# Moving DMA issue, weight casts and eviction copies between engines in the Q and K stage of a fused attention and Mish block

## The chip, the cores and the metric

The kernel runs on one core of a Trainium2 chip. The metric is the device time of one execution in microseconds (us). Engines are named as in the profile: PE (TensorE, matmuls), PEld (its weight loads), DVE (VectorE), ACT (ScalarE), POOL (GpSimd) and SP (SyncE, which only issues transfers). SPq and ACTq are the sequencers of SP and ACT, where DMA issues appear.

## The reference

The input x is 2048 x 1024. It is normalised by row, and two branches use the result:

```
x  = A_x
xn = layernorm(x)
s  = attention(xn, A_wqkv, 32 heads of 32) @ A_wo
h  = xn @ B_w1 + B_b1                  # 1024 -> 3584
g  = silu((h * tanh(softplus(h))) @ B_w2)   # 3584 -> 1024
out = x + s * g
```

All inputs are float32.

## The kernel before

**Precision.** A matmul in one pass of float32r is not exact enough, so operands are split into a high part (a copy that rounds to float32r) and a low part (the value minus its high part). The helper `copy` (line 275) makes a high part on ACT, `low` (line 282) the low part on the engine that it is given, and `THREE` (line 286) is the list of the three products high x high, high x low, low x high that are added up in PSUM. `move` (line 278) issues a DMA, on SP unless it is given another engine.

**Stages.** First the rows of x are normalised, transposed and split, and V is made, with the first splits of W1 beside it. Then comes the Q and K stage, where the change lies. Then a planner (`Plan`, line 84) lays out by costs the instructions of attention and of the two dense layers; its order doesn't depend on the run. Last comes the output projection.

**The Q and K stage** is the loop at line 709. The 16 values of f are 128-column blocks of the Q and K weights, in turn Q and K; c runs over four blocks of 512 rows. `qk_group(f, c)` (line 692) is a *group*: 24 matmuls (8 slices of 128 by `THREE`) into one PSUM tile `ps` of one bank, out of eight banks; the high part copied out to `qst`, the low part subtracted from it on DVE, and a store of 512 KB to the DRAM tensors `qs` or `ks`. Groups are numbered here from 0 to 63 as 4f + c.

The weights of a block are loaded by `qk_load(f)` (line 478) into `qkraw` (one buffer), and split by `qk_split(f)` (line 484), which calls `split_w` (line 348), into `qkw` (two buffers in turn). The split of block f + 1 is put after group (f, 0), and the load of block f + 2 right after that.

From f = 12, each group is followed by four score matmuls of head 0 (`s_mm`, line 580), each with a bank of its own and a maximum on DVE (line 586); `m_tail` (line 590) turns the maxima into rows of the Q operand. Head 0's Q and K are loaded at f = 8, head 1's at f = 15 (`load_head`, line 562).

**The work beside it.** A list `todo` holds splits of weights that the dense layers need later: `presplit` (line 632) for the last blocks of W1, and `w2_parts` (line 657) for W2. W2 is split for a fast product with seven combinations of four quarters: per double block u there are four steps with 2, 2, 2 and 1 combinations. `minus` forms a combination on POOL where one is needed (four times per u), and `w2_part` (line 651) casts and subtracts on POOL into a tile `pw`, which is stored by SP one tick later. The list of 108 units of work is laid out by a due group, `cost / PACE`, so many units per group; the loop takes what is due after each group. `later` holds what is to be issued some groups (ticks) later. `pw_tile` (line 627) takes tiles in turn from two places, three buffers each.

Each engine, and each DMA queue, works in the order in which the program issues to it. In this stage ACT issues the stores of `qst` and the loads of `qkraw` (from f = 2); SP issues everything else.

Of the kernel before, what the change touches and what calls it, by code (L numbers as in the profile page):

```python
# [10 lines left out]
F32R = mybir.dt.float32r  # L11
# [7 lines left out]
P = 128  # L19
# [6 lines left out]

W1_0, W1_V = 4, 23

PACE = 1.85
NS = H * NT  # L30
U = FT // 2

# [191 lines left out]
def body(ctx: ExitStack, tc: tile.TileContext, x, wqk, wv, wo, w1, b1, w2, out):  # L224
    nc = tc.nc
# [6 lines left out]
    def pool(stack, name, bufs, side="left", **kw):  # L232
        return stack.enter_context(tc.tile_pool(name=name, bufs=bufs, side=side, reuse_waits="tile", **kw))
# [9 lines left out]
    w2s = [dram.tile([P, 7, 2, 512], F32R, name=f"w2s{i}") for i in range(U)]  # L243
# [25 lines left out]
    w1p = pool(low_, "w1p", 1)  # L269
# [5 lines left out]
    def copy(out_, in_, scale=1.0):  # L275
        nc.scalar.activation(out_, in_, AF.Copy, scale=scale)  # L276

    def move(out_, in_, eng=None):

        (eng or nc.sync).dma_start(out_.bitcast(F32), in_.bitcast(F32))  # L280

    def low(eng, out_, in_, high):

        eng.tensor_tensor(out_, in_, high.bitcast(F32), ALU.subtract)  # L284
# [10 lines left out]
    later = Later()  # L295
# [52 lines left out]
    def split_w(w, raw, job=False):  # L348
        for half in range(2):
            r = slice(half * 4, half * 4 + 4)  # L350
            p = w[half] if isinstance(w, list) else w[:, half]
            if job:
                nc.gpsimd.tensor_copy(p[:, 0], raw[:, r])
            else:
                copy(p[:, 0], raw[:, r])
            low(nc.gpsimd if job else nc.vector, p[:, 1], raw[:, r], p[:, 0])

    def w1_first(n, step):
        t, g = xc[2 + n // 2], n % 2
        raw = first_w1[n // 2][:, g]  # L360
        w = t[:, 1, 4 * g:4 * g + 4].rearrange("p k n -> p (k n)") \
            .rearrange("p (h a k f) -> p h a k f", h=2, a=2, f=P)
        if step == 0:
            nc.sync.dma_start(raw, w1[n])
        elif step == 1:
            split_w(w, raw, True)
        else:
            move(w1s[n], w)
# [75 lines left out]
    for t in range(2, NT + 2):  # L444
# [22 lines left out]
        if t > 7:  # L467
            c, k = t // 4 - 1, t % 4 * 2
# [7 lines left out]
    raws = {}  # L476

    def qk_load(f):
        raws[f] = big.tile([P, KT, P], F32, tag="raw", name=f"qkraw{f}")
        (nc.scalar if f > 1 else nc.sync).dma_start(raws[f], wqk[f])  # L480

    qkw = {}

    def qk_split(f):
        qkw[f] = w_tile(f"qkw{f}")
        split_w(qkw[f], raws.pop(f))
# [4 lines left out]
    def w1_early(step):  # L491
        f, late = W1_0 + step // 2, step % 2
        if not late:
            if f < W1_V:
                raw = vp.tile([P, KT, P], F32, tag="x", name=f"w1e{f}", bufs=5)
                nc.sync.dma_start(raw, w1[f])
                early_w1[f] = raw
            if W1_0 < f <= W1_V:
                f -= 1
                raw = early_w1.pop(f)  # L500
                if f % 3 == 2:
                    w = [w1p.tile([P, 2, KT // 2, P], F32R, tag="w1", name=f"w1h{f}_{i}", bufs=3) for i in range(2)]
                    split_w(w, raw, True)
                    early_w1[f] = [(w1s[f][:, i], w[i]) for i in range(2)]
                else:
                    w = w_tile(f"w1p{f}")
                    split_w(w, raw, True)
                    early_w1[f] = [(w1s[f], w)]
        elif W1_0 < f <= W1_V:
            for args in early_w1.pop(f - 1):  # L510
                move(*args)

    for i in range(1, 4):
        vw = nvw
        for t in range(NT):
            v_group(i, vw, t)()
            w1_early((i - 1) * NT + t)
            if t == 4 and i < 3:
                nvw = v_split(i + 1, vraw)
                if i < 2:  # L520
                    vraw = v_load(i + 2)
            if i == 3 and t == 1:
                qk_load(0)
            if i == 3 and t == 7:
                qk_split(0)
                qk_load(1)
# [6 lines left out]
    qst, kst = [], []  # L533
# [88 lines left out]
    sp = pool(qb, "sp", 2, side="right")  # L622
    jobs = iter([(f, half) for f in range(W1_V, FT) for half in range(2)])

    pw_made = []

    def pw_tile(name):
        pw_made.append(name)
        where, tag = ((w1p, "w1"), (sp, "pw"))[len(pw_made) % 2]
        return where.tile([P, 2, 512], F32R, tag=tag, name=name, bufs=3)  # L630

    def presplit():
        f, half = next(jobs)
        raw = sp.tile([P, 512], F32, tag="praw", name=f"praw{f}_{half}", bufs=1)
        nc.sync.dma_start(raw.rearrange("p (k f) -> p k f", f=P), w1[f][:, half * 4:half * 4 + 4])

        def split():
            w = pw_tile(f"pw{f}_{half}")
            nc.gpsimd.tensor_copy(w[:, 0], raw)
            low(nc.gpsimd, w[:, 1], raw, w[:, 0])  # L640
            later.at(1, lambda: move(w1s[f][:, half], w.rearrange("p a (k f) -> p a k f", f=P)))

        later.at(2, split)
# [3 lines left out]
    def w2_load(u):  # L647
        raw2[u] = early.tile([P, 4, 512], F32, tag=f"{'qk'[u % 2]}stack1", name=f"raw2_{u}")
        nc.sync.dma_start(raw2[u].rearrange("p (f d) n -> p f (d n)", f=2), w2[u])

    def w2_part(u, j, v):
        w = pw_tile(f"pw2_{u}_{j}")
        nc.gpsimd.tensor_copy(w[:, 0], v)
        low(nc.gpsimd, w[:, 1], v, w[:, 0])
        later.at(1, lambda: move(w2s[u][:, j], w))

    def w2_parts(u, step):
        b11, b12, b21, b22 = [raw2[u][:, i] for i in range(4)]
        if step == 0:
            raw2[u, "t"] = sp.tile([P, 512], F32, tag="tmp2", name=f"tmp2_{u}", bufs=1)  # L660
        tmp = raw2[u, "t"]

        def minus(a, b, out_):
            nc.gpsimd.tensor_tensor(out_, a, b, ALU.subtract)
            return out_

        if step == 0:
            w2_part(u, 0, b11)
            w2_part(u, 2, b21)
        elif step == 1:  # L670
            w2_part(u, 5, minus(b12, b11, tmp))
            w2_part(u, 1, minus(b22, b12, b12))
        elif step == 2:
            w2_part(u, 4, minus(b22, tmp, tmp))
            w2_part(u, 6, b22)
        else:
            w2_part(u, 3, minus(b21, tmp, tmp))

    todo, cost = [], 0.0
    for u in range(U):  # L680
        for step, n in enumerate((2, 2, 2, 1)):
            def job(u=u, step=step):
                w2_parts(u, step)
                if step == 3 and u + 2 < U:
                    later.at(1, lambda: w2_load(u + 2))
            todo.append((cost / PACE, job))
            cost += n
        if u < 2 * (FT - W1_V):
            todo.append((cost / PACE, presplit))
            cost += 1  # L690

    def qk_group(f, c):
        w = qkw[f]
        ps = ps1.tile([P, 512], F32, tag="ps", name=f"qk{f}_{c}")
        n = 0
        for k in range(KT):
            for a, b in THREE:
                nc.tensor.matmul(ps, w[:, k // 4, a, k % 4], xc[c][:, b, k], start=n == 0, stop=n == 3 * KT - 1)  # L698
                n += 1
        st = sp.tile([P, 2, 512], F32R, tag="qst", name=f"qst{f}_{c}")  # L700
        copy(st[:, 0], ps)
        low(nc.vector, st[:, 1], ps, st[:, 0])
        dst = (qs, ks)[f % 2][f // 2].rearrange("h p n -> p h n")[:, :, c * 512:(c + 1) * 512]
        move(dst, st, nc.scalar)

    w2_load(0)
    w2_load(1)
# [1 line left out]
    for f in range(2 * KT):  # L709
        for c in range(NC):  # L710
            qk_group(f, c if f < 2 * KT - 1 else (c + 1) % NC)
            while todo and todo[0][0] <= f * NC + c:
                todo.pop(0)[1]()
            if c == 0 and f + 1 < 2 * KT:
                qk_split(f + 1)
                if f + 2 < 2 * KT:
                    later.at(1, lambda f=f + 2: qk_load(f))
            if f == 8 and c == 0:
                load_head(0)
            if f == 15 and c == 0:  # L720
                stacks(early, 1)
                load_head(1)
            if f >= 12:
                for kc in range(4):
                    s_mm(0, 4 * (f - 12) + c, kc)
            if f == 2 * KT - 1 and c == 1:
                load_w1(0)
                load_w1(1)
            later.tick()
# [489 lines left out]
    wt, ohl, ps, wo_loads, wo_ops, o_ops, o_first = {}, {}, {}, {}, {}, {}, []  # L1219
# [250 lines left out]
```

## Time and profile before

| | |
|---|---|
| median of three runs | 3464.68 us (3463.0 to 3465.96) |
| the profiled execution | 3463.9 us |
| its span in the trace | 3462.1 us |
| mean granted PE clock | 0.992 |
| busy over the span | PE 97%, POOL 81%, DVE 76%, ACT 58% |
| moved by DMA | 639.92 MB, mean 185 GB/s |

The span is the time from the first to the last instruction on the core; 1.8 us of the execution lie outside it. The Q and K stage takes about an eighth of it. Its rows are shown where the argument uses them. In a row of the waits the numbers are the total in us, how often, and the longest; the arrow points to what ended the wait. In a row of an instruction group they are the busy time, the mean ns of one, and the idle time just before them with its releasers. In the order of time they are start and duration in us.

### The profile page before, as it was taken

To read this page: it belongs to the slowest core of one execution; us is meant where nothing else is said; L and a number is where in the kernel's file an instruction comes from. 1 tells how busy PE (TensorE), PEld (TensorE's weight loads), DVE (VectorE), ACT (ScalarE), POOL (GpSimd) and SP (SyncE) were. 2 spreads that over 40 slices of the span, in tenths; PEclk is the share of its full clock that TensorE was granted. 3 is DMA by queue.
4 is the path that set the end of the run, shared out by engine and by line. 5 is a ranking of instruction groups with operands and counts; after the bars stand their busy time and mean duration, and the time that the engine had idled before them with its cause. 6 is when DMAs were issued, how large, how long until landed. Compare 5 with 4: busy or idle time off the path is not lost. (4 is left out here: it accounts for less than half of the span.)

```text
span 3462.1 us, 48685 instructions
## 1 busy us (share of the span) xinstructions
PE 3371.6 (97%) x17491; PEld 2473.6 (71%) x17491; DVE 2619.2 (76%) x4382; ACT 2020.3 (58%) x3360; POOL 2792.6 (81%) x1033
## 2 busy tenths in 40 slices
PE   8999898999999999999999999999999999999999
PEld 7998676767776666667677676666676666667687
DVE  6011214799999998888989988898999889996753
ACT  6111111576776666767767667676676676677621
POOL 2669891589888888989889889989988999999910
PEclk9999999999999999999999999999999999999999
DMA  9889994444555556545445654445545545556582
GB/s 333 326 302 348 343 354 160 139 139 135 153 155 152 156 157 204 153 138 151 143 144 157 191 178 146 128 141 151 154 147 189 177 135 154 151 159 192 167 307 85
DMA packets 255477, 639.92 MB, mean 185 GB/s; under 512 B 90026, under 2 KB 99242, under 8 KB 244906
## 3 DMA queue, kind: packets, MB, share of 16 engines
q1 hardware_dynamic: 233364, 587.52, 54.3%
q10 hardware_dynamic: 21872, 49.29, 3.8%
q8 instruction: 139, 2.28, 0.3%
q14 instruction: 102, 0.84, 0.1%
HBM read 474.97 MB, written 160.69 MB: 184 GB/s over the span
## 5 line engine op out<-in xcount | busy, mean ns | idle before, releaser
L889 POOL TENSOR_TENSOR z<-z,p 128x2048 f32<-128x2048 f32 x448 | 2067.0, 4614 | 76.3 <-ACT p L273 51.4
L273 ACT ACTIVATE p<-t,zero 128x512 f32<-128x512 f32 x2048 | 1366.6, 689 | 459.7 <-PE t L860 439.4
L779 DVE TENSOR_REDUCE mx<-s 128x1 f32<-128x512 f32 x1984 | 1284.0, 682 | 70.2 <-PE s L773 67.5
L860 PE MATMUL t<-qstack,kstack 128*128 128x512 f32 x2048 | 791.5, 394 | 4.4 <-DMA qstack<-mt 2.7
L773 PE MATMUL s<-kstack,qstack 128*128 128x512 f32 x1984 | 755.8, 397 | 15.6 <-DMA kstack<-ks 5.9
L1019 PE MATMUL h<-xr,w 128*128 128x512 f32 x2016 | 678.3, 391 | 1.4 <-DVE aw L284 0.6
L1183 DVE TENSOR_TENSOR yacc<-yacc,y 128x512 f32<-128x512 f32 x728 | 492.6, 680 | 38.9 <-PE y L1160 35.7
L773 PEld LDWEIGHTS s<-kstack,qstack 128*128 128x128 f32 x1984 | 367.4, 188 | 161.5 <-issue 29.4
L860 PEld LDWEIGHTS t<-qstack,kstack 128*128 128x128 f32 x2048 | 381.7, 188 | 129.4 <-issue 31.6
L908 PE MATMUL pv<-p,v 128*32 128x512 f32 x4096 | 466.6, 596 | 0.9 <-ACT p L273 0.6
L1019 PEld LDWEIGHTS h<-xr,w 128*128 128x128 f32 x2016 | 378.7, 188 | 84.6 <-DVE aw L284 2.1
L698 PE MATMUL qk<-xc,qkw 128*128 128x512 f32 x1536 | 362.5, 397 | 20.8 <-ACT qkw L276 18.6
L698 PEld LDWEIGHTS qk<-xc,qkw 128*128 128x128 f32 x1536 | 294.1, 192 | 86.4 <-ACT qkw L276 20.3
L889 POOL TENSOR_TENSOR z<-p,p 128x2048 f32<-128x2048 f32 x32 | 147.8, 4619 | 237.9 <-ACT p L273 130.5
L908 PEld LDWEIGHTS pv<-p,v 128*32 128x32 f32 x4096 | 120.0, 110 | 276.8 <-issue 247.5
L284 DVE TENSOR_TENSOR qst<-qk,qst 128x512 fp32r<-128x512 f32 x64 | 44.3, 692 | 261.5 <-ACT qst L276 261.5
L1160 PE MATMUL y<-w,az 128*128 128x512 f32 x672 | 232.6, 396 | 4.0 <-DMA w<-w2s 2.6
L1160 PE MATMUL y<-w,ay 128*128 128x512 f32 x672 | 228.4, 393 | 3.3 <-ACT ay L276 1.3
L1160 PE MATMUL y<-w,ax 128*128 128x512 f32 x672 | 225.4, 392 | 2.8 <-DVE ax L284 0.7
L276 ACT ACTIVATE qst<-qk 128x512 fp32r<-128x512 f32 x64 | 38.3, 599 | 321.5 <-PE qk L698 118.7
L1019 PE MATMUL h<-xc,w 128*128 128x512 f32 x672 | 224.9, 390 | 0.7 <-DVE mx L586 0.7
L331 PE MATMUL v<-vw,xc 128*128 128x256 f32 x1536 | 192.9, 286 | 5.9 <-DVE xc L284 3.7
(123 smaller groups left out, 3664.3 us busy)
## 6 DMA issues: line engine op xcount, KB each, us to landing
w<-w2s SPq DMA_DIRECT2D x392, 512.0 KB
w<-w1s SPq DMA_DIRECT2D x224, 512.0 KB
w2s<-pw SPq DMA_DIRECT2D x98, 512.0 KB
qstack<-qs SPq DMA_DIRECT2D x96, 256.0 KB
kstack<-ks SPq DMA_DIRECT2D x96, 256.0 KB
x<-in_A_x_dram SPq DMA_DIRECT2D x32, 512.0 KB
qs<-qst ACTq DMA_DIRECT2D x32, 512.0 KB
ks<-qst ACTq DMA_DIRECT2D x32, 512.0 KB
```

The source lines that it names most:

```text
L273: nc.scalar.activation(out_, in_, fn, bias=zero if bias is None else bias, scale=scale)
L284: eng.tensor_tensor(out_, in_, high.bitcast(F32), ALU.subtract)
L331: nc.tensor.matmul(ps[:, :256], xc[t // 4][:, a, k, (t % 4) * P:(t % 4 + 1) * P], w[:, b, k], start=n == 0, stop=n == 3 * KT - 1)
L698: nc.tensor.matmul(ps, w[:, k // 4, a, k % 4], xc[c][:, b, k], start=n == 0, stop=n == 3 * KT - 1)
L773: nc.tensor.matmul(sp_, qst[h % 3][:, qt * P:(qt + 1) * P], kst[h % 3][:, kc * 512:(kc + 1) * 512], start=True, stop=True)
L779: nc.vector.reduce_max(tiles["mx"][:, qt, kc:kc + 1], tiles[qt, kc], axis=AX.X)
L860: nc.tensor.matmul(tp, kst[h % 3][:, kt * P:(kt + 1) * P], qst[h % 3][:, c * 512:(c + 1) * 512], start=True, stop=True)
L889: nc.gpsimd.tensor_tensor(zs[h], pts[T - 1] if kt == 1 else zs[h], pts[T], ALU.add)
L908: nc.tensor.matmul(t["b"][c * DH:(c + 1) * DH, :], vt[h][:, k, :], pts[T - kt + k][:, c * 512:(c + 1) * 512], start=k == kt - size + 1, st ...
L1019: nc.tensor.matmul(t["h"], w1t[m_][:, a, k % 4], xts_[c][:, b, k], start=i == 0, stop=i == 3 * KT - 1)
L1160: nc.tensor.matmul(t["y"], acts[B, kind][:, p, half * 256 + s * P:half * 256 + (s + 1) * P], w2t[m_][:, q], start=i == 0, stop=i == 2)
L1183: nc.vector.tensor_tensor(ya, ya, t["y"], ALU.subtract)
```

## The change

In the Q and K stage:

- ACT issues no DMA: the stores of `qst` and all loads of `qkraw` go to SP's queue.
- `split_w` outside the early jobs makes the high parts of the Q and K weights on DVE instead of ACT; the low parts were on DVE already.
- The high part of a group's output is copied out by DVE for f below 12, and by ACT, as before, from f = 12.
- The high parts of W2's combinations, and of the W1 blocks in `presplit`, are made by ACT instead of POOL. POOL keeps the combinations and the low parts. Within a step of W2, all combinations and high parts are now put out before the low parts; step 2 does its two combinations in the other order.
- `qst` has three buffers instead of two. The tiles `pw` have five instead of six: two in one place, three in the other.
- `PACE` is 1.9 instead of 1.85, and the due times start at a cost of 2 instead of 0.

```
-PACE = 1.85
+PACE = 1.9
...
-            if job:
-                nc.gpsimd.tensor_copy(p[:, 0], raw[:, r])
-            else:
-                copy(p[:, 0], raw[:, r])
+            (nc.gpsimd if job else nc.vector).tensor_copy(p[:, 0], raw[:, r])
             low(nc.gpsimd if job else nc.vector, p[:, 1], raw[:, r], p[:, 0])
...
-        (nc.scalar if f > 1 else nc.sync).dma_start(raws[f], wqk[f])
+        nc.sync.dma_start(raws[f], wqk[f])
...
-        where, tag = ((w1p, "w1"), (sp, "pw"))[len(pw_made) % 2]
-        return where.tile([P, 2, 512], F32R, tag=tag, name=name, bufs=3)
+        where, tag, bufs = ((w1p, "w1", 3), (sp, "pw", 2))[len(pw_made) % 5 % 2]
+        return where.tile([P, 2, 512], F32R, tag=tag, name=name, bufs=bufs)
...
             w = pw_tile(f"pw{f}_{half}")
-            nc.gpsimd.tensor_copy(w[:, 0], raw)
+            copy(w[:, 0], raw)
             low(nc.gpsimd, w[:, 1], raw, w[:, 0])
...
-    def w2_part(u, j, v):
+    def w2_high(u, j, v):
         w = pw_tile(f"pw2_{u}_{j}")
-        nc.gpsimd.tensor_copy(w[:, 0], v)
-        low(nc.gpsimd, w[:, 1], v, w[:, 0])
-        later.at(1, lambda: move(w2s[u][:, j], w))
+        copy(w[:, 0], v)
+
+        def rest():
+            low(nc.gpsimd, w[:, 1], v, w[:, 0])
+            later.at(1, lambda: move(w2s[u][:, j], w))
+
+        return rest
...
         if step == 0:
-            w2_part(u, 0, b11)
-            w2_part(u, 2, b21)
+            lows = [w2_high(u, 0, b11), w2_high(u, 2, b21)]
         elif step == 1:
-            w2_part(u, 5, minus(b12, b11, tmp))
-            w2_part(u, 1, minus(b22, b12, b12))
+            minus(b12, b11, tmp)
+            minus(b22, b12, b12)
+            lows = [w2_high(u, 5, tmp), w2_high(u, 1, b12)]
         elif step == 2:
-            w2_part(u, 4, minus(b22, tmp, tmp))
-            w2_part(u, 6, b22)
+            minus(b22, tmp, tmp)
+            lows = [w2_high(u, 6, b22), w2_high(u, 4, tmp)]
         else:
-            w2_part(u, 3, minus(b21, tmp, tmp))
-
-    todo, cost = [], 0.0
+            minus(b21, tmp, tmp)
+            lows = [w2_high(u, 3, tmp)]
+        for fn in lows:
+            fn()
+
+    todo, cost = [], 2.0
...
-        st = sp.tile([P, 2, 512], F32R, tag="qst", name=f"qst{f}_{c}")
-        copy(st[:, 0], ps)
+        st = sp.tile([P, 2, 512], F32R, tag="qst", name=f"qst{f}_{c}", bufs=3)
+        if f < 12:
+            nc.vector.tensor_copy(st[:, 0], ps)
+        else:
+            copy(st[:, 0], ps)
         low(nc.vector, st[:, 1], ps, st[:, 0])
...
-        move(dst, st, nc.scalar)
+        move(dst, st)
```

More of the change, by code (lines that the diff above doesn't have):

```diff
@@ L664, in minus @@
             nc.gpsimd.tensor_tensor(out_, a, b, ALU.subtract)
-            return out_
         if step == 0:
-            w2_part(u, 0, b11)
-            w2_part(u, 2, b21)
+            lows = [w2_high(u, 0, b11), w2_high(u, 2, b21)]
         elif step == 1:
-            w2_part(u, 5, minus(b12, b11, tmp))
-            w2_part(u, 1, minus(b22, b12, b12))
+            minus(b12, b11, tmp)
+            minus(b22, b12, b12)
+            lows = [w2_high(u, 5, tmp), w2_high(u, 1, b12)]
         elif step == 2:
-            w2_part(u, 4, minus(b22, tmp, tmp))
-            w2_part(u, 6, b22)
-        else:
-            w2_part(u, 3, minus(b21, tmp, tmp))
-    todo, cost = [], 0.0
+            minus(b22, tmp, tmp)
+            lows = [w2_high(u, 6, b22), w2_high(u, 4, tmp)]
+        else:
+            minus(b21, tmp, tmp)
[3 more added lines that the diff above has]
+    todo, cost = [], 2.0
     for u in range(U):
```

## The prediction

> **What bounds the kernel now.** I read the page first, then the busy times by stretch, then PE's order of time at the end of the Q and K stage, then the waits of that stage.
>
> ```profile
> span 3462.1 us, 48685 instructions
> PE 3371.6 (97%) x17491; PEld 2473.6 (71%) x17491; DVE 2619.2 (76%) x4382; ACT 2020.3 (58%) x3360; POOL 2792.6 (81%) x1033
> PE   8999898999999999999999999999999999999999
> 220.00:340.00 120.00, 120.00 (x531) 99.35 (x530) 28.83 (x34) 18.05 (x31) 103.74 (x101) 1.00 0.92 336
> 340.00:420.00 80.00, 65.47 (x263) 51.69 (x262) 16.81 (x18) 10.11 (x18) 69.74 (x67) 0.91 0.94 330
> 420.00:500.00 80.00, 80.00 (x354) 66.25 (x353) 16.93 (x19) 11.60 (x20) 74.06 (x73) 1.00 0.99 371
> 500.00:540.00 40.00, 20.32 (x68) 14.74 (x67) 9.73 (x13) 4.95 (x9) 33.04 (x33) 0.75 0.83 304
> 540.00:630.00 90.00, 90.00 (x391) 74.31 (x390) 46.48 (x80) 11.90 (x23) 0.00 (x0) 0.98 0.38 124
> ```
>
> PE, busy for 97% of the span, is the bound almost everywhere. The digits dip where the Q and K stage lies, and the stretches (columns: length, then PE, PEld, DVE, ACT and POOL busy with counts, granted clock, DMA share, GB/s) say how: PE is full in three of them and loses time in 340 to 420 and 500 to 540, with a lower granted clock (0.91, 0.75) in the same two. The stage can therefore be shortened only by what it loses there. To price that:
>
> ```profile
> L698 PE MATMUL qk<-xc,qkw x1536: 387/389/796, 219.8 to 629.0; 128*128 128x512 f32 x192
> 617.45 5.60 PE L698 MATMUL qk<-xc,qkw 128*128 128x512 f32 x24
> 622.89 1.07 PE L582 MATMUL s<-kstack,qstack 128*128 128x512 f32 x4
> 623.80 5.60 PE L698 MATMUL qk<-xc,qkw 128*128 128x512 f32 x24
> 630.15 0.33 PE L559 MATMUL mtp<-ident_r,hl 128*128 128x128 f32 x2
> ```
>
> Near the end PE runs without a gap: a group of 24 matmuls and four for scores take 623.80 - 617.45 = 6.35 us, so one matmul costs 6.35 / 28 = 0.2268 us and a group alone 24 x 0.2268 = 5.44 us. The stage's 64 groups and their 64 score matmuls (16 groups with four each) need 1600 x 0.2268 = 362.9 us. The stage runs from 219.8 to 630.15, 410.35 us. So **47.5 us are lost**, clock included. That is the whole prize: 1.4% of the span.
>
> What PE waits for is at one remove. PE runs ahead of ScalarE by the eight PSUM banks, then stops for ScalarE:
>
> ```profile
> ACT qst L276 <- PE qk L698: 107.2, 23, 8.7
> ACT qst L276 <- DMA w2s<-pw: 68.3, 14, 7.3
> ACT qst L276 <- DMA ks<-qst: 47.3, 8, 10.0
> ACT qst L276 <- DMA qs<-qst: 43.8, 8, 8.3
> ACT qkw L276 <- DMA w2s<-pw: 13.9, 3, 7.2
> PE qk L698 <- ACT qkw L276: 18.6, 4, 6.9
> 515.79 10.69 SPq L280 DMA_DIRECT2D w2s<-pw  x5
> 518.47 0.37 ACTq L280 DMA_DIRECT2D ks<-qst  x1
> 518.94 0.60 ACT L276 ACTIVATE qst<-qk 128x512 fp32r<-128x512 f32 x1 [7.25 <-DMA w2s<-pw]
> 525.61 0.37 ACTq L280 DMA_DIRECT2D ks<-qst  x1
> 526.08 0.60 ACT L276 ACTIVATE qst<-qk 128x512 fp32r<-128x512 f32 x1 [6.53 <-DMA w2s<-pw]
> ```
>
> The copy's 107.2 us for PE are harmless: ScalarE was early. Its 47.3 and 43.8 us are for its own older stores, which hold the two qst tiles. But it also waits 68.3 us, 14 times, for w2s<-pw, a transfer that touches none of its operands. The order of time shows why: at 518.47 ScalarE issues a store (ks<-qst), and only then comes the copy, after 7.25 us of idling. The store, not the copy, had been held until a W2 transfer of SyncE's queue landed. The same happens at 525.61. So stores on ScalarE's queue are tied to SyncE's transfers, those to POOL's splits, and the copies stand behind the stores; the qkw copies that PE needs stand there too.
>
> **The change, part by part.** *ScalarE issues nothing.* All 64 qst stores and 14 weight loads leave its queue, so its copies can no longer stand behind a held store. The 68.3 and 13.9 us of waits for w2s lose their place. A store can still be held, but now SyncE is held, and nobody computes there.
>
> *VectorE does more.* Rows for its pieces:
>
> ```profile
> L284 DVE TENSOR_TENSOR qst<-qk,qst 128x512 fp32r<-128x512 f32 x62 | 42.9, 692 | 255.0 <-ACT qst L276 255.0
> L284 DVE TENSOR_TENSOR qkw<-qkraw,qkw 128x512 fp32r<-128x512 f32 x30 | 34.7, 1196 | 28.7 <-ACT qkw L276 18.0 <-DMA w2s<-pw 10.6
> L260 DVE CAST ident_r<-ident 128x128 fp32r<-128x128 f32 x1 | 0.2, 227 | 0.4 <-POOL ident masks.py:199 0.4
> L586 DVE TENSOR_REDUCE mx<-s 128x1 f32<-128x512 f32 x56 | 34.7, 681 | 0.0
> ```
>
> It gains 48 eviction copies (f below 12) and 32 weight copies. Neither is in the trace at this size; an eviction copy reads PSUM as the subtraction does, so I take 0.69. A weight copy lies between the cast of 128 columns, 0.23, and four times it, 0.91; I take 0.7. For one f below 12: 4 x (0.69 + 0.69) + 2 x (0.7 + 1.2) = 9.3 us of 4 x 5.44 = 21.8. For f from 12: 4 x 0.69 + 16 x 0.68 + 3.8 = 17.4 of 25.4. Neither binds, so the cost on the path is nothing; PE covers it. At 0.91 it is 0.4 more per f and the cover holds.
>
> *POOL loses its casts.*
>
> ```profile
> L284 POOL TENSOR_TENSOR pw<-raw,pw 128x512 fp32r<-128x512 f32 x56 | 73.6, 1315 | 4.5
> L653 POOL CAST pw<-raw 128x512 fp32r<-128x512 f32 x56 | 37.0, 661 | 19.0 <-DVE qst L284 17.0 <-DMA w1s<-pw 1.0
> L653 POOL CAST pw<-tmp 128x512 fp32r<-128x512 f32 x42 | 27.1, 644 | 2.7
> L639 POOL CAST pw<-praw 128x512 fp32r<-128x512 f32 x10 | 6.6, 657 | 13.8 <-DMA praw<-in_B_w_dram 13.8
> L276 ACT ACTIVATE qkw<-qkraw 128x512 fp32r<-128x512 f32 x30 | 17.3, 623 | 29.6 <-DMA w2s<-pw 13.9 <-DVE qst L284 13.0 <-DMA w1s<-pw 2.6
> ```
>
> The splits come in 108 units (98 of W2, 10 of W1). POOL is busy 103.74 + 69.74 + 74.06 + 33.04 = 280.6 us for them, 2.60 a unit. Without 37.0 + 27.1 + 6.6 = 70.7 us of casts it is 1.94. At 1.9 units a group that is 3.7 us of 5.44, where it was 1.85 x 2.60 = 4.8. ScalarE makes 108 casts at 0.62 (the qkw row), 67 us over the stage, and drops 48 evictions and 32 weight copies; it has no other work below f = 12.
>
> *One line for all transfers.* SyncE now issues the store of group g, then the W2 stores that were queued with group g, in program order. Each W2 store waits for POOL's subtraction, and the next qst store stands behind it. Two limits decide whether that reaches PE. The first is bytes:
>
> ```profile
> w2s<-pw SPq DMA_DIRECT2D x98, 512.0 KB
> raw<-in_B_w_dram SPq DMA_DIRECT2D x14, 1024.0 KB
> qkraw<-in_A_wqk_dram ACTq DMA_DIRECT2D x14, 512.0 KB
> w1s<-pw SPq DMA_DIRECT2D x10, 512.0 KB
> praw<-in_B_w_dram SPq DMA_DIRECT2D x10, 256.0 KB
> ```
>
> A unit moves (98 x 0.524 + 14 x 1.049 + 10 x 0.786) / 108 = 0.684 MB; a group adds its 0.524 MB store and a quarter of a weight load, 0.131. At 1.9 units that is 1.955 MB per 5.44 us, 359 GB/s, and 307 GB/s from f = 12. Between 420 and 500 the trace carried 371 GB/s with PE full; between 220 and 340 it was 336, at a share of 0.92, so not yet at its limit. I take it that 359 fits, barely. The second limit is the life of a pw tile. There are five instead of six, and 1.9 are used per group, so each may live 5 / 1.9 x 5.44 = 14.3 us. It lives through a cast (0.62), one or two subtractions (1.3 to 2.6), the issue and the landing. A W2 store landed in 518.47 - 515.79 = 2.7 us when little was under way; for the loaded case:
>
> ```profile
> 399.06 0.37 ACTq L280 DMA_DIRECT2D qs<-qst  x1
> 408.11 0.60 ACT L276 ACTIVATE qst<-qk 128x512 fp32r<-128x512 f32 x1 [3.39 <-DMA qs<-qst]
> ```
>
> That store took 9.05 us. So a life is 5 to 12.6 us, under 14.3. Three qst tiles instead of two allow a store three groups, 16 us.
>
> The Trainium skill, "DMA: Bandwidth & Descriptors", section "Queues, rings and completion order", speaks against the change here: each DMA engine takes turns between queue rows, so a store on ScalarE's row shares with SyncE's backlog, while in one row it stands behind all of it. By that rule a loaded landing grows from 9.05 us by about one group's bytes, 1.955 MB / 371 GB/s = 5.3 us, to 14.3, a life of 17.9; no run here shows it, and the sum below keeps the measured 9.05.
>
> *From f = 12* ScalarE evicts again and also casts. A cast that waits for a free tile holds the eviction behind it, and the banks cover less there (five are used per group). About ten groups (48 to 57) hold such casts. The bounds are 0 and 6.3 us each (12.6 of life less one group's 6.35, where three tiles fall on one group and a tile is wanted again after one); most come after two or three groups, 12.7 to 19 us, so I take 0.3 each, 3 us together. The burst of six head loads at f = 8 I put at 2 us, between none and the 7 us that PE lost there before (the 6.9 in the qkw row). PACE and the initial cost of 2 move the last split from group 58 (107 / 1.85) to 57.4 (109 / 1.9): nothing. Head 1's loads, which before ran ten groups early, now come at group 60, some 19 us before the stage ends; landing in 9 leaves cover.
>
> **The sum.** 3463.9 (the profiled execution, 0.8 below the median) - 47.5 + 3 + 2 = 3421.4. With the 0.8 for the median, **3422 us**, 1.2% faster. Bounds of the unknowns: 3417 with no stall, 3432 if they come to 15.
>
> **The rivals.** *Transfers take over the pace.* For: the DMA share of 0.92 to 0.99. Against: 371 GB/s beside a full PE. Up to group 57 the line carries 108 x 0.684 + 58 x 0.655 + 1.6 (head 0) = 113.5 MB; at 336 GB/s that is 338 us against 48 x 5.44 + 10 x 6.35 = 324.6, so 13 us more: 3435. At 320 GB/s 30 more, 3452.
>
> *The one line is latency-bound, and slower.* The place is SyncE's order: a qst store behind a W2 store behind POOL behind a cast behind a landing. If a tile lives L, a group takes L / 2.63. It decides from L = 14.3, and eats the whole gain where 58 groups lose 47.5 us, at 0.82 more a group, L = 16.5. At L = 18 a group takes 6.84, 1.4 more, over 48 groups 67 us: 3422 + 67 = 3489. Against it: it needs landings of 14 us, and 9.05 is what the loaded trace shows. The skill's rule on rows, above, would give L = 17.9, this case.
>
> *The change frees nothing.* If the 68.3 us of waits are only ScalarE arriving early, PE's stalls stay and VectorE waits in ScalarE's place: 3464, give or take 6. Against it: 18.6 us of PE's waits are for exactly those copies.
>
> **How the numbers follow.** Forecast 0.62 (3416 to 3432), transfers 0.24 (3432 to 3457), nothing freed 0.06, latency-bound 0.08. A run tells 0.2%, 7 us, from no change. Faster: 0.86; same: 0.06; slower: 0.08. The range from 3416 to 3447 leaves out the slow cases and the far end of the transfer case, about 0.2.
>
> **What would show it.** Right: the qk matmuls end near 585, PE full from 220 to 580 with a granted clock of 1.00, no eviction waiting for w2s<-pw, POOL busy some 210 us there with gaps, 350 GB/s or more up to 550. Wrong: VectorE's qst copies waiting for ks<-qst or qs<-qst with a DMA share of 1.00 (transfers), POOL's subtractions waiting for ScalarE's casts and those for w2s<-pw (latency), or PE waiting for VectorE's qkw. PE stalls between 500 and 560 would mean that I priced the casts among the evictions too low.

## The result, and the profile after

The changed kernel takes 3418.24 us (median of four runs, 3416.96 to 3419.64) against 3463.84 for the kernel before beside it: 45.6 us less, a ratio of 0.9868 with a 95% interval of 0.9851 to 0.9885. The forecast was 3422. The profiled execution took 3416.96 us, its span is 3415.2.

The same stretches as before, and the rows that bound the Q and K stage (line 698 is now 701, 582 is 579):

```profile
220.00:340.00 120.00, 120.00 (x531) 99.36 (x530) 58.12 (x71) 24.13 (x40) 76.91 (x58) 1.00 0.90 339
340.00:420.00 80.00, 80.00 (x355) 66.24 (x354) 35.86 (x43) 16.09 (x27) 53.69 (x40) 1.00 0.97 350
420.00:500.00 80.00, 79.61 (x351) 65.35 (x350) 40.38 (x50) 18.35 (x30) 57.04 (x44) 1.00 0.99 379
500.00:540.00 40.00, 39.62 (x174) 32.26 (x173) 25.30 (x38) 9.70 (x19) 20.95 (x16) 1.00 0.73 283
540.00:590.00 50.00, 47.38 (x208) 38.36 (x207) 32.54 (x52) 7.94 (x19) 9.52 (x7) 1.00 0.61 200
```

```profile
L701 PE MATMUL qk<-xc,qkw x1536: 387/389/500, 219.7 to 584.3; 128*128 128x512 f32 x192
585.40 0.33 PE L556 MATMUL mtp<-ident_r,hl 128*128 128x128 f32 x2
```

PE is full from 220 on, at a granted clock of 1.00, and the stage ends at 585.40. It lasts 585.40 - 219.7 = 365.7 us, where the matmuls alone need 362.9. So 44.65 of the 47.5 us came back; the other 2.3 us of the spans' 46.9 lie outside the stage.

The waits of the stage in the kernel after:

```profile
DVE qst L705 <- PE qk L701: 120.4, 35, 4.0
ACT qst L276 <- PE qk L701: 65.7, 13, 5.7
ACT pw L276 <- DMA w2s<-pw: 40.6, 26, 7.2
DVE qst L705 <- DMA qs<-qst: 3.8, 1, 3.8
DVE qst L705 <- DMA ks<-qst: 3.3, 1, 3.3
PE s L579 <- DVE mx L583: 0.9, 3, 0.3
```

The evictions now wait almost only for PE, as they should. ScalarE still waits for W2 stores, but with a cast, not with an eviction. One row per kernel tells more than these. It is the W2 stores, with their first and last start, of the kernel before and of the one after:

```profile
L280 SPq DMA_DIRECT2D w2s<-pw x98: 319/320/853, 228.9 to 534.5; - x98
```

```profile
L280 SPq DMA_DIRECT2D w2s<-pw x98: 319/479/1977, 238.1 to 555.3; - x98
```

And these are the matmuls of Q and K from the last of those stores on, again before and after:

```profile
L698 PE MATMUL qk<-xc,qkw x336: 389/389/796, 538.4 to 629.0; 128*128 128x512 f32 x168
```

```profile
L701 PE MATMUL qk<-xc,qkw x113: 389/389/447, 555.1 to 584.3; 128*128 128x512 f32 x113
```

Before, W2 was finished with 336 / 24 = 14 groups still to run, though its last unit was due at group 58 of 64, with six to go. After, it finishes with 113 / 24 = 4.7 groups to go. The prediction did not look at that.

### The profile page after: what moved, and what is told of

Its sections match the earlier page's. It is cut to its first block, busy times and chain, and to the rows that moved or that the text cites. A ratio compares the mean times of both kernels' runs of the same rounds, so it can differ in the third digit from the quotient of the medians.

```text
span 3415.2 us, 48772 instructions
## 1 busy us (share of the span) xinstructions
PE 3357.6 (98%) x17491; PEld 2466.6 (72%) x17491; DVE 2688.2 (79%) x4462; ACT 2038.6 (60%) x3388; POOL 2730.8 (80%) x925
## 5 line engine op out<-in xcount | busy, mean ns | idle before, releaser
L701 PE MATMUL qk<-xc,qkw 128*128 128x512 f32 x1536 | 351.3, 389 | 0.3
L331 PEld LDWEIGHTS v<-vw,xc 128*128 128x128 f32 x1536 | 187.4, 193 | 8.8 <-DVE xc L284 5.5
L926 DVE TENSOR_TENSOR o<-o,pv 128x512 f32<-128x512 f32 x96 | 65.9, 687 | 116.8 <-PE pv L914 113.1
```

Source lines behind the costliest of these rows:

```text
L331: nc.tensor.matmul(ps[:, :256], xc[t // 4][:, a, k, (t % 4) * P:(t % 4 + 1) * P], w[:, b, k], start=n == 0, stop=n == 3 * KT - 1)
```

## The experiments

The working theory was the prediction's: ScalarE's copies stood behind stores that it had to issue, and those were held (the *queue* theory). The rival was that the gain is POOL's relief from its casts (called the POOL theory in the expectations). The first four runs took parts of the change alone or undid them. All ratios are to the kernel before on the same chip, which had medians of 3461.63, 3460.45 and 3458.9 us in the three sets.

**Only the queue changed.**

```
 before.py, the loads and stores of the stage:
-        (nc.scalar if f > 1 else nc.sync).dma_start(raws[f], wqk[f])
+        nc.sync.dma_start(raws[f], wqk[f])
...
-        move(dst, st, nc.scalar)
+        move(dst, st)
```

> The kernel before, with one part of the change alone: the qst stores and the qkraw loads go to SyncE's queue. POOL keeps its casts, ScalarE its copies, two qst tiles, six pw tiles, PACE 1.85. Queue theory (ScalarE's copies stood behind stores that were held until transfers of SyncE's queue had landed): nearly the whole gain, 3418 to 3432 us, and no eviction copy waiting for w2s<-pw for longer than its tile needs. POOL theory (the gain is the 70.7 us of casts taken from POOL, which set the pace of the stores): 3455 to 3465 us.

3411.06 us, ratio 0.9858 (0.9843 to 0.9873), 7 us below the range given for the queue theory. The queue alone gives all of the gain; POOL's casts, ScalarE's copies and two qst tiles may stay. Its waits:

```profile
ACT qst L276 <- PE qk L698: 199.1, 42, 6.6
ACT qst L276 <- DMA ks<-qst: 52.3, 10, 7.8
ACT qst L276 <- DMA qs<-qst: 41.8, 9, 12.2
```

The waits for ScalarE's own older stores, 94.1 us, are as long as before (91.1) and cost PE nothing. Those for w2s<-pw are gone.

**The queue change undone.** The changed kernel with those two lines back.

```
 after.py:
-        nc.sync.dma_start(raws[f], wqk[f])
+        (nc.scalar if f > 1 else nc.sync).dma_start(raws[f], wqk[f])
...
-        move(dst, st)
+        move(dst, st, nc.scalar)
```

> The changed kernel with that part undone: the qst stores and the qkraw loads from f = 2 are issued by ScalarE again, all else as changed. Queue theory: the stores held on ScalarE now hold the W2 casts behind them, and with those POOL; the gain is gone, 3450 to 3475 us. POOL theory: POOL is still relieved and VectorE still evicts, so 3418 to 3428 us.

3416.3 us, ratio 0.9871 (0.9856 to 0.9886). The gain stays; the time is 1.7 us below the range given for the rival and far from the one for the queue theory. The queue theory as stated falls: ScalarE may issue. But POOL's relief isn't the cause either, as the first run showed. In this run ScalarE makes the W2 casts in its own order, behind its stores:

```profile
ACT pw L276 <- DVE qst L284: 116.4, 31, 17.8
POOL pw L284 <- ACT pw L276: 113.3, 39, 30.9
```

The casts wait for the groups' subtractions, and POOL waits for the casts.

**VectorE makes the copies, the queues as before.**

```
 before.py, in split_w:
-            if job:
-                nc.gpsimd.tensor_copy(p[:, 0], raw[:, r])
-            else:
-                copy(p[:, 0], raw[:, r])
+            (nc.gpsimd if job else nc.vector).tensor_copy(p[:, 0], raw[:, r])
... in qk_group:
-        copy(st[:, 0], ps)
+        nc.vector.tensor_copy(st[:, 0], ps)
```

> The kernel before with the high parts of the Q and K weights and of all 64 outputs made by VectorE, so that ScalarE has nothing but the stores and loads to issue in most of the stage; the queues are as before. It splits the queue theory in two. If the harm was that copies stand behind held stores in ScalarE's order, it is gone: 3420 to 3435 us. If the harm is the held store itself, which keeps one of only two qst tiles, VectorE now waits where ScalarE waited: 3450 to 3466 us, with VectorE's qst copies waiting for landings.

3461.35 us, ratio 1.000 (0.999 to 1.001). No copy that PE waits for stands behind a store any more, and nothing is gained:

```profile
DVE qst L698 <- DMA qs<-qst: 95.2, 14, 14.9
DVE qst L698 <- DMA ks<-qst: 64.7, 14, 13.5
PE qk L695 <- DVE qkw L352: 14.1, 3, 9.1
```

VectorE now waits where ScalarE waited, for tiles that the held stores keep. The held store itself is the harm, not what stands behind it.

**POOL casts again, one queue.** The changed kernel with `nc.gpsimd.tensor_copy` in place of `copy` in `presplit` and `w2_high`.

> The changed kernel with the high parts of W2 and of the late W1 blocks cast by POOL again, all transfers on SyncE. POOL then needs some 2.6 us a unit, 4.9 of the 5.44 us of a group. Queue theory: it still fits, 3416 to 3428 us. POOL theory: 3450 us or more.

3414.44 us, ratio 0.9867 (0.985 to 0.9885), 1.6 us below the range of the queue theory: POOL's relief is worth nothing.

**A theory that fits all four.** In the kernel before nothing ties the splits to the groups. POOL reads only loaded weights, SyncE's line holds little but their transfers, and the due times only fix the program's order on each engine. So the splits can run ahead at POOL's own speed. The trace names the semaphore that each transfer signals on completion; there are eight, taken in turn by the transfers of both queues, and a transfer is issued only when the last one on its semaphore has landed. The stores that ScalarE issued at 518.47, 525.61, 529.77 and 534.77 each came 0.08 us after the landing of a W2 store (issued at 515.79, 522.93, 526.17 and 531.30) that signals on the same semaphore. Followed through both queues, that turn puts 106 of the 108 split stores ahead of group 45's store, the one issued at 518.47, where 1.85 x 45 = 83 are due. So late in the stage ScalarE's stores wait for transfers whose pace POOL sets.

One line for all transfers ties the two together, since a W2 store comes behind the store of its group; casts in ScalarE's order do too. By the same count 81 units stand ahead of that store in the kernel after, in the run with the queue alone and in the run with it undone, but 105 in the one with VectorE's copies. This *run-ahead* theory says that any tie will do, and no other part matters much. Its main rival is that the third qst tile made the gain. The next four runs test it.

**A tie and nothing else.**

```
 before.py, at the end of qk_group:
         move(dst, st, nc.scalar)
+        tie = sp.tile([P, 8], F32, tag="tie", name=f"tie{f}_{c}", bufs=1)
+        nc.gpsimd.tensor_copy(tie, st[:, 1, :8].bitcast(F32))
```

> The kernel before with its queues, engines, buffers and pace as they were, and one small POOL instruction added per group: a copy of 8 columns of the group's finished qst tile into a scratch tile, ahead of the weight splits that are put out after that group. It leaves nothing out; it only keeps POOL, and with it the W2 stores, from running ahead of the groups. Run-ahead theory (in the kernel before the splits are done up to ten groups early, since nothing ties POOL or SyncE's queue to the groups, and stores of ScalarE take turns behind those early transfers): nearly the whole gain, 3412 to 3428 us, with ScalarE still issuing and still copying. Any theory that puts the gain on which engine issues, casts or copies, or on the third qst tile: 3455 us or more, POOL having some 6 us more to do.

3421.86 us, ratio 0.9884 (0.9868 to 0.9901). ScalarE issues, copies and has two tiles, as before; POOL has more to do; and 0.0116 of the changed kernel's 0.0132 are there. The stores, and the Q and K matmuls after the last of them:

```profile
POOL tie L706 <- DVE qst L284: 58.9, 12, 17.4
L280 SPq DMA_DIRECT2D w2s<-pw x98: 319/320/1015, 228.7 to 563.0; - x98
L698 PE MATMUL qk<-xc,qkw x97: 389/389/447, 562.8 to 588.3; 128*128 128x512 f32 x97
```

POOL waits 58.9 us for groups, W2 ends with four groups to go, and by the count above 82 units stand ahead of group 45's store, not 106.

**Both ties cut.** The changed kernel with the edits of the second and the fourth run together.

> The changed kernel with stores and loads back on ScalarE and the W2 and W1 casts back on POOL; VectorE's copies, three qst and five pw tiles, PACE 1.9 and the later start stay. Neither SyncE's line nor ScalarE's order now ties the splits to the groups. Run-ahead theory: the gain is gone, 3448 to 3466 us. If a third qst tile, the pace or VectorE's copies made it: 3414 to 3425 us.

3447.01 us, ratio 0.9961 (0.9946 to 0.9976). Each of these edits alone cost nothing; together they lose 70% of the gain ((0.0132 - 0.0039) / 0.0132), at 1 us below the range expected for that.

```profile
500.00:540.00 40.00, 17.23 (x64) 13.14 (x64) 15.75 (x23) 2.39 (x4) 22.48 (x23) 0.70 0.87 287
L280 SPq DMA_DIRECT2D w2s<-pw x98: 319/320/1340, 229.8 to 523.0; - x98
L701 PE MATMUL qk<-xc,qkw x336: 387/389/792, 524.8 to 614.5; 128*128 128x512 f32 x168
```

The old hole at 500 to 540 is back (PE busy 17.23 of 40 us, clock 0.70), again 336 matmuls are left, and the count is 105. The third qst tile, the pace and VectorE's copies stay as changed in this run, so they hold at most the other 30%.

**Casts on ScalarE alone**, in the kernel before.

> The kernel before with the casts of W2 and the late W1 blocks on ScalarE, nothing else: two qst tiles, stores on ScalarE, in its order behind the evictions. Run-ahead theory: ScalarE's order is the tie, so most of the gain, 3412 to 3432 us. Theory of three tiles: 3445 us or more.

3433.19 us, ratio 0.9923 (0.9908 to 0.9937): the tie works (108 matmuls left, a count of 82), with 27 us gained, just beyond the range. What keeps the other 18 wasn't isolated; here ScalarE makes casts, evictions and weight copies behind two qst tiles, and PE waits 10.6 us for VectorE's maxima, against 0.9 in the changed kernel.

**POOL slowed.** Each cast of a split in the kernel before is done twice.

> The kernel before with every cast of a split on POOL done twice, 0.65 us more a unit, 70 us over the stage; results are the same. If PE's stalls came from a full DMA (bytes per us), the splits now ask for fewer bytes per us and the time stays or falls: 3440 to 3464 us. If ScalarE's stores wait for their turn behind W2 stores, whose pace POOL sets, the stalls grow with POOL's time: 3490 to 3535 us.

3522.35 us, ratio 1.018 (1.0165 to 1.0195).

```profile
ACT qst L276 <- DMA w2s<-pw: 116.0, 14, 17.8
PE qk L700 <- ACT qkw L276: 54.4, 6, 12.7
L280 SPq DMA_DIRECT2D w2s<-pw x98: 319/320/419, 230.1 to 599.5; - x98
L700 PE MATMUL qk<-xc,qkw x336: 387/389/793, 598.9 to 688.9; 128*128 128x512 f32 x168
```

Some 70 us more on POOL, an engine off PE's path by data, cost 62 us. A full DMA can't be the cause, since fewer bytes were asked for per us. The same 336 matmuls are left, at a count of 103, although POOL is far slower: the turn is laid down with the program, and the run has to keep to it. So the stalls come from the order laid down, and POOL's speed sets how long they last. Why that order runs so far ahead of the due times in the source isn't shown by any run. Nor was the turn changed by itself: a tie changes the turn and also holds POOL back, and no run does only one of the two. In all four untied kernels (before, VectorE's copies, both ties cut, POOL slowed) the last Q and K matmul starts 89 to 95 us after the last W2 store (534.5 to 629.0, 539.7 to 628.5, 523.0 to 614.5, 599.5 to 688.9), the time of 14 groups at 6.35 us, 88.9. POOL set the end of the stage.

**What the other parts are worth.** The last four ran on one chip.

> The changed kernel itself, on the chip and beside the runs of the other three, so that differences of a few us can be told: 3414 to 3420 us.

3415.7 us, ratio 0.9871 (0.9857 to 0.9886), for the changed kernel itself.

> The kernel before with all transfers of the stage on SyncE, three qst and five pw tiles, PACE 1.9, the later start and the new order of a W2 step; ScalarE makes all copies of Q and K, POOL all casts. The split moved to ScalarE and the copies moved to VectorE are thus left out. If these two add nothing: no slower than the changed kernel, 3408 to 3418 us. If they are worth their place: 3422 us or more.

3412.52 us, 0.9860 (0.9845 to 0.9876): moving casts and copies between engines adds nothing.

> The changed kernel, but from f = 13 on the high parts of the Q and K weights are made by ScalarE. VectorE's weight copies took 1.1 us on average, not the 0.7 that was put down for them, and four times PE had to wait about 0.9 us there for VectorE's maxima. If those copies are the cause, the stage gets 2 to 3 us shorter: 3412 to 3416 us. If the subtractions alone hold the maxima, no difference.

```
 after.py, in split_w, put shortly, for f from 13 on:
+            copy(p[:, 0], raw[:, r])          # instead of nc.vector.tensor_copy
```

3414.14 us, 0.9871 (0.9854 to 0.9887).

```profile
L704 PE MATMUL qk<-xc,qkw x1536: 389/389/447, 219.8 to 581.5; 128*128 128x512 f32 x192
582.61 0.33 PE L559 MATMUL mtp<-ident_r,hl 128*128 128x128 f32 x2
```

In its profile the stage lasts 582.61 - 219.8 = 362.8 us, 2.9 less than in the changed kernel and no more than its matmuls need, and the waits of its score matmuls for VectorE's maxima are gone. So few us are too little for the times to tell.

> The changed kernel with two qst tiles instead of three, five pw tiles as changed. If the third tile carries part of the gain: 3 to 15 us slower, with VectorE's qst copies waiting for landings of qs<-qst and ks<-qst. If the eight banks cover it: no difference.

3412.53 us, 0.9865 (0.9851 to 0.9880): the third tile carries nothing once the ties are there. None of these is told from the changed kernel by its interval, so there is no version shown to be faster. The smallest that gets the gain is the first run, two lines.

## Why the prediction was right, and where not

*The prize* was right: 47.5 us lost in the stage, of which 44.65 came back.

*The stalls left over* were put at 5 and measured at 365.7 - 362.9 = 2.8, but not where they were put. The casts among the evictions were to cost 3 and the head loads 2: both cost nothing. What is lost lies in three places of 0.9 us each (at 493.76, 520.11 and 546.45), where VectorE's copies of the weights of f = 13, 14 and 15 hold up the maxima; with those copies on ScalarE the loss was gone (362.8 us). The mis-sized term is that copy, put at 0.7 us between 0.23 and 0.91:

```profile
L352 DVE CAST qkw<-qkraw 128x512 fp32r<-128x512 f32 x30 | 33.4, 1112 | 0.0
L705 DVE CAST qst<-qk 128x512 fp32r<-128x512 f32 x48 | 33.1, 690 | 136.0 <-PE qk L701 120.4 <-DMA w1s<-pw 4.4 <-DMA praw<-in_B_w_dram 4.0
```

It takes 1.11 on average, beyond the upper bound, because it waits for POOL (see the last section); four that met no POOL instruction took 0.41. The eviction copy was put at 0.69 and takes 0.690.

Of the 4.4 us between the 3421.4 of the sum and the 3416.96 of the profiled execution, about half are these stalls, and the other half lies outside the stage, where the sum put no change.

*The mechanism* was half right. That stores were held until W2 stores landed, at a pace set by POOL, is what the runs show. That the gain would come because ScalarE's copies no longer stand behind them is the step that failed: freeing the copies alone gave nothing (ratio 1.000), and leaving ScalarE its stores cost nothing (0.9871). The rival that VectorE would wait in ScalarE's place was given 0.06 as a case for the whole change; for that part by itself it is what happened. What worked is in the same paragraphs, as a risk: SyncE's line makes W2 stores wait behind the groups. That the forecast is so close is partly luck: the sum takes the whole prize, whatever gives it back, and this change happens to hold a tie.

*POOL's relief* was worked out about rightly (1.94 us a unit; 218.10 us busy from 220 to 590, where some 210 were put) but is worth nothing to the time.

*PACE* was said to move nothing. In the kernel before it couldn't: the splits didn't keep to it. In the changed kernel they do, but the first run, at the old 1.85, is no slower.

*Bytes and one line.* 359 GB/s were held to fit, barely. The kernel after carries 379 between 420 and 500 beside a PE at 79.61 of 80 us. The transfer rival and the latency rival both fell: VectorE's evictions wait no more than 4.0 us at a time for any landing. The rule on queue rows from the Trainium skill ("DMA: Bandwidth & Descriptors", "Queues, rings and completion order") would have stretched a tile's life to 17.9 us and cost PE; no such cost shows here. The same page of the Trainium skill states under "Issuing engines are not separate DMA queues" that a second issuing engine saves little but issue time; this fits the first run, where leaving that engine out cost nothing.

## What to carry to other kernels

Work that fills gaps beside a main loop should be tied to that loop's progress by something that the engines really wait for; a due time in the program's order ties nothing when the filler has its own engine and queue. When an engine waits for a transfer that touches none of its operands, look for what orders the two, and compare how far each stream has come at the same moment. Undo a part of a change as well as trying it alone: either tie here hides what the other does.

## What the runs showed of the hardware

VectorE's weight copy took from 413 to 1531 ns for one shape; four that no POOL instruction overlapped took 414 to 416. The order of time shows how, with VectorE's rows and POOL's from the kernel after:

```profile
487.72 1.53 DVE L352 CAST qkw<-qkraw 128x512 fp32r<-128x512 f32 x1
489.29 1.66 DVE L284 TENSOR_TENSOR qkw<-qkraw,qkw 128x512 fp32r<-128x512 f32 x1
490.87 1.51 DVE L352 CAST qkw<-qkraw 128x512 fp32r<-128x512 f32 x1
492.41 0.69 DVE L284 TENSOR_TENSOR qkw<-qkraw,qkw 128x512 fp32r<-128x512 f32 x1
```

```profile
487.68 1.29 POOL L284 TENSOR_TENSOR pw<-tmp,pw 128x512 fp32r<-128x512 f32 x1 [0.47 <-ACT pw L276]
488.93 1.47 POOL L284 TENSOR_TENSOR pw<-raw,pw 128x512 fp32r<-128x512 f32 x1
490.36 1.74 POOL L665 TENSOR_TENSOR tmp<-raw,tmp 128x512 f32<-128x512 f32 x1
```

The two engines take turns: the cast begun at 487.72 ends at 489.25, after POOL's subtraction ended at 488.97; POOL's next, begun at 488.93, ends at 490.40. VectorE's subtraction between the two copies takes 1.66 us; the last one, with POOL idle from 492.10, takes 0.69. The Trainium skill, "SBUF — State Buffer", section "Who interferes with whom", says that a VectorE copy in a two-port mode and a GpSimd instruction exclude each other for a whole instruction; this trace agrees that the two exclude each other, with 413 ns at the least and 1.1 us on average, while the mode of a copy is not in it. The eviction copy, which reads PSUM, took 676 to 692 ns in all 48 cases.
